# First layer from the fourth batch on as seven half-size products

## The chip, the cores and the metric

The kernel runs on one core of one Trainium2 chip. The metric is the device time of one execution in microseconds: the median of 3 runs before is 1244.26 us (1241.83 to 1246.42). Every time below is from the profiled execution, which has a time of its own.

## What is computed

Attention over 8 batches and 12 heads, with RMS-normed queries and keys, and then a two-layer network over all tokens:

```python
q_n, k_n = rmsnorm(q, g_q), rmsnorm(k, g_k)          # (8, 12, 448, 64)
attn = softmax(q_n @ k_n.T / sqrt(64))
x = (attn @ v)                                       # as (3584 tokens, 768)
h = x @ w_in                                         # (3584, 2048)
g = where(h > 0, h, exp(min(h, 0)) - 1)
return g @ w_out                                     # (3584, 768)
```

The inputs and outputs are float32.

## The kernel before

**Numbers in halves.** The matrix multiplies run on float16 operands. A float32 operand is kept as a high and a low half, and a product takes three matmuls into one bank: high by high, high by low, low by high. Weights are scaled by powers of two (`conv`, `conv_in`, `conv_out`, which run in the first 250 us or so beside the first two batches). First-layer weights stay on chip as `whi` and `wli`, 16 tiles each of six 128x128 blocks. High halves of the second layer stay as `whos`; its low halves go to DRAM (`wl_d`) and come back for every batch as `wls` (`wl_load`).

**Work of a batch.** A batch is 448 tokens. Attention of a batch has six pairs of heads, each with seven tiles of 128 rows of scores, 42 tiles. A tile T: `s_mm` makes scores in one of four banks (`t_s`; five in the first batch); DVE takes the maximum (`s_max`); ACT the exponential (`s_exp`); POOL, DVE, ACT and DVE turn it into two halves of probabilities `p` (`s_z`, `s_rec`, `s_hi`, `s_lo`; three buffers); SP transposes them by DMA into `ptall` (`s_tr`). After seven tiles `attend` multiplies a pair with v into the bank `av`, and `x_high` and `x_low` read from it one chunk of x in halves (a ring of nine chunks, `xs`). The network of batch b runs while attention of batch b+1 does (`mlp`). Its first layer makes 16 columns f of 128 features: 6 chunks x 3 matmuls of 448 tokens into one of three banks (`t_mo`: m0, m1 and s4); then the ELU steps of `m1_out`: an exponential on ACT, a subtraction and a maximum on DVE (which reads the bank last), and the halves `gall` by ACT and DVE. Its second layer makes six outputs d of 16 x 3 matmuls and reads each bank by ACT (`m2_out`). After the last batch's attention the network runs alone.

**The order.** No scheduler moves anything: a loop over half-steps h (two per tile, 84 per batch, HB) emits each step where the tables in SCHED put it, and each engine runs its own list in that order. From the third batch on the tables repeat a pattern. How many matmuls of the network are due by h is told by `due`, from the table "rate" and then at an even rate of 576 a batch. What couples the engines is the banks, the buffers named above and SP's single list of transfers.

```python
for i, (w, r) in enumerate(((wh, 0), (wh, 1), (wl, 0))):
    last = c == NC_ - 1 and i == 2
    nc.tensor.matmul(
        ph[:, :S], w[:, c, :], x[:, r, :], start=(c == 0 and i == 0), stop=last
    )
    yield m1_out(b, f, ph) if last else None
```

## Time and profile before

| | |
|---|---|
| median of 3 runs | 1244.26 us |
| profiled execution, its own time | 1245.14 us |
| span of the profile | 1243.4 us |
| mean granted TensorE clock | 0.995 |
| PE busy | 1188.5 us, 96%, 7180 matmuls |
| DVE, ACT, POOL busy | 866.0, 809.9, 498.9 us (70%, 65%, 40%) |
| DMA queue of SP | 413280 packets, 208.22 MB, 74.5% of 16 engines' span |

PE's row of the page counts a matmul from its first read to a modelled end, so two that follow each other overlap; a stage's pace is the distance of their starts. PEld is the weight load, which has a row of its own. "x288" and the like are counts. An arrow behind an idle time names what ended it. SPq is SP's own list: the time that an entry holds the list, not the time that the data takes.

### The profile page before, as it was taken

Reading aid. Unit: us, or ns where it says so; the run is one execution under the profiler, and the core shown is the slowest. Engines: PE = TensorE matmul, PEld = TensorE weight load, DVE = VectorE, ACT = ScalarE, POOL = GpSimd, SP = SyncE. Lnnn points to the kernel's source line nnn. Section 1 sums busy time; section 2 is a strip of 40 time slices with the busy share of each in tenths; the row PEclk is TensorE's granted clock in tenths of the full one; section 3 lists DMA queues with packets and bytes.
Section 4 is the critical chain, followed back from the end, with each engine's and each line's share of the span. In section 5 each row is a group of like instructions: output and inputs, shape, how many; then the busy total and the mean of one; then the engine's idle time right before and its main releaser. Section 6 shows DMA issues by size and latency. Waiting matters only on the chain.

```text
span 1243.4 us, 21717 instructions
## 1 busy us (share of the span) xinstructions
PE 1188.5 (96%) x7180; PEld 735.9 (59%) x7180; DVE 866.0 (70%) x2042; ACT 809.9 (65%) x1705; POOL 498.9 (40%) x789
## 2 busy tenths in 40 slices
PE   3878899999999999999999999999999999999998
...
GB/s 301 225 197 156 213 205 227 172 249 191 142 162 186 227 135 162 167 206 182 152 143 199 214 138 162 157 230 167 145 151 197 213 139 166 126 154 71 1 50 64
DMA packets 413393, 209.62 MB, mean 169 GB/s; under 512 B 369504, under 2 KB 389600, under 8 KB 413280
## 3 DMA queue, kind: packets, MB, share of 16 engines
q1 hardware_dynamic: 413280, 208.22, 74.5%
q8 instruction: 57, 0.93, 0.3%
...
## 4 chain that ended last, share of the span: by engine, by line
PE 77%; DVE 2%; DMA 2%; ACT 1%; issue 0%; POOL 0%; ACTq 0%
PE m L757 21%; PE m L743 21%; PE s L757 11%; PE s L743 10%; PE s L542 8%; PE av L635 7%; DMA ptall<-p 2%; DVE p L608 1%; ACT p L603 0%; ACT s L563 0%; DVE w32s L268 0%; DVE st L549 0%; DVE gall L692 0%; DVE w32s L314 0%; DVE e L679 0%
## 5 line engine op out<-in xcount | busy, mean ns | idle before, releaser
L549 DVE TENSOR_REDUCE st<-s 128x1 f32<-128x448 f32 x336 | 207.2, 619 | 158.7 <-PE s L542 156.3
L757 PE MATMUL m<-gall,whos 128*128 128x448 f16 x1024 | 282.0, 353 | 0.0
L567 POOL TENSOR_SCALAR st<-st 128x1 f32<-128x1 f32 x294 | 73.6, 250 | 488.6 <-ACT s L563 478.9
L757 PEld LDWEIGHTS <-whos 128*128 128x128 f16 x1536 | 221.7, 144 | 73.4 <-issue 0.7
L743 PE MATMUL m<-x,whi 128*128 128x448 f16 x926 | 256.0, 352 | 1.6 <-DVE x L649 1.2
L563 ACT ACTIVATE s<-s,st 128x448 f32<-128x448 f32 x294 | 178.1, 606 | 93.5 <-DVE st L549 90.3
L603 ACT ACTIVATE p<-s,st 128x448 f16<-128x448 f32 x294 | 185.1, 631 | 71.6 <-DMA ptall<-p 49.5
L743 PEld LDWEIGHTS <-whi 128*128 128x128 f16 x1536 | 149.7, 98 | 138.5 <-issue 3.6
L608 DVE SCALAR_TENSOR_TENSOR p<-s,st,p 128x448 f16<-128x448 f32 x294 | 198.5, 676 | 30.0 <-ACT p L603 29.2
L542 PE MATMUL s<-qkt 128*128 128x448 f16 (+1 forms) x768 | 185.4, 360 | 18.1 <-DMA qkt<-qkt 5.4
L757 PE MATMUL m<-gall,wls 128*128 128x448 f16 x512 | 181.3, 354 | 0.0
L743 PE MATMUL m<-x,wli 128*128 128x448 f16 x463 | 163.5, 353 | 0.0
L757 PE MATMUL s<-gall,whos 128*128 128x448 f16 x512 | 140.9, 353 | 0.0
L757 PEld LDWEIGHTS <-wls 128*128 128x128 f16 x768 | 110.6, 144 | 41.5 <-issue 6.8
L743 PE MATMUL s<-x,whi 128*128 128x448 f16 x450 | 124.0, 352 | 0.7 <-DVE e L679 0.7
L743 PEld LDWEIGHTS <-wli 128*128 128x128 f16 x768 | 75.1, 98 | 74.4 <-issue 7.0
L542 PEld LDWEIGHTS <-qkt 128*128 128x128 f16 (+1 forms) x768 | 63.3, 101 | 82.0 <-issue 36.8
L689 ACT ACTIVATE gall<-e,ui 128x448 f16<-128x448 f32 x128 | 85.1, 665 | 31.8 <-DVE e L684 31.8
L635 PE MATMUL av<-ptall,vt 128*64 128x448 f16 x924 | 96.9, 357 | 1.7 <-DMA ptall<-p 1.1
L692 DVE SCALAR_TENSOR_TENSOR gall<-e,ui,gall 128x448 f16<-128x448 f32 x128 | 87.7, 686 | 8.5 <-ACT gall L689 8.3
L387 POOL TENSOR_TENSOR nat<-nat,r 128x896 f32<-128x896 f32 (+1 forms) x48 | 84.5, 1760 | 22.3 <-DVE r L377 13.0
L757 PE MATMUL s<-gall,wls 128*128 128x448 f16 x256 | 90.6, 354 | 0.0
...
## 6 DMA issues: line engine op xcount, KB each, us to landing
wls<-wl_d SPq DMA_DIRECT2D x48, 512.0 KB, 4.1
...
raws<-in_w_out SPq DMA_DIRECT2D x24, 512.0 KB, 4.3
...
```

What stands on the lines that cost most here:

```text
L387: nc.gpsimd.tensor_tensor(out=n[:, a:], in0=n[:, a:], in1=r[:, a:], op=ALU.mult)
L542: nc.tensor.matmul(ps[r0 : r0 + n, :S], lhs, qq[:, 1, h * S : h * S + S], start=(t == 0), stop=(t == 2),)
L549: nc.vector.tensor_reduce(out=st[:, 0:1], in_=pss[T][:, :S], axis=AX.X, op=ALU.max, negate=True)
L563: nc.scalar.activation(e, ps, AF.Exp, bias=st[:, 0:1], accum_out=st[:, 1:2])
L567: (nc.vector if by_pe(T) else nc.gpsimd).tensor_scalar(out=st[:, 1:2], in0=st[:, 1:2], scalar1=1e-9, scalar2=2.0 ** (UP - 7) if by_pe(T) e ...
L603: nc.scalar.activation(p16[:, :S], pss[T][:, :S], AF.Copy, scale=stats[T][:, 2:3])
L608: nc.vector.scalar_tensor_tensor(out=p16[:, S:], in0=ps[:, :S], scalar=r, in1=p16[:, :S], op0=ALU.mult, op1=ALU.subtract)
L635: nc.tensor.matmul(av[64 * h : 64 * h + 64, :S], vs[:, h], ps[h], start=(k == 0), stop=(k == len(terms) - 1),)
L689: nc.scalar.activation(g[:, 0], e, AF.Copy, scale=ui)
L692: nc.vector.scalar_tensor_tensor(out=g[:, 1], in0=e, scalar=ui, in1=g[:, 0], op0=ALU.mult, op1=ALU.subtract)
L743: nc.tensor.matmul(ph[:, :S], w[:, c, :], x[:, r, :], start=(c == 0 and i == 0), stop=last)
L757: nc.tensor.matmul(py[:, :S], w, g[:, r, :], start=(f == 0 and i == 0), stop=last)
```

## The change

**Seven products.** From batch 3 (`FROM`), that is the fourth, the first layer is computed two columns at a time (`first`; eight pairs g). The 448 tokens are cut in two halves of 224, the six chunks of x in even and odd ones, and the two columns are the other cut of the weights, so that a pair is a 2x2 block product. It is made from seven products of sums of quarters instead of eight. A product is 3 chunk pairs x 3 terms of 224 tokens, 9 matmuls; two products share a bank (`ORDER7`), so a pair takes four turns of the three banks, and 63 matmuls. The rate table counts two of them as one.

**Adding them up.** `combine` reads each bank when it is done: two copies on ACT, five additions on DVE, two on POOL without a bank, into `quad` (two buffers) and `two` (one). The ELU steps then read from there, as they do in the first batch: the Relu is on ACT in place of the subtraction on DVE.

**Sums of x.** `x_even` and `x_odd` take the place of `x_high` and `x_low`: copies of `av` into `mix` by ACT, three subtractions on POOL for two chunks, and halves of seven pieces in place of four (448 and 1120 elements a row).

**Sums of weights.** `ratios` and `blocks` make, once, four sums of quarters for each pair, between half-steps 160 and 272 (batches 2 and 3 of attention). Two columns now share a scale, which adds a maximum of one column for every odd column while the weights are converted. High halves of three sums stay on chip (`wsum`); their low halves go to DRAM (`sl_d`) and are fetched for each product, 24 transfers of 96 KB a batch into four buffers (`fetch`), each behind the product that used the buffer last. The fourth sum replaces a quarter of `whi` and `wli` during batch 2's second layer (`fetch_sum`, 16 transfers).

**Tables.** From the third batch on, new tables give each step of a batch a place of its own ("tile+", "qk+", "v+", "mm+", "att+", "rate+"). The first layer of a batch now runs from half-step 12 to 50 of 84. After the last attention the steps advance every 3 counts in place of 7. Buffers of the conversion are put in one tile `work`, which the sums use afterwards.

```diff
 
     def t_s(T):
-        return sb[T % (5 if T < PB + 5 else 4)]
-
-    def t_mo():
+        return sb[T % (5 if T < PB + 5 else 4 if T < FROM * PB + PB else NSB)]
+
+    def t_mo(n=3):
         nonlocal taken
-        taken += 1
-        return mb[(taken - 1) % 3]
+        i = taken % n
+        taken = i + 1
+        return (mb + [sb[3]])[i]
...
-    xs = [const.tile([128, 2, S], F16, name=f"x{i}") for i in range(NX - 1)]
+    xall = const.tile([128, (NX - 1) * 2 * S], F16, name="xall")
+    xs = [t.rearrange("p (i s) -> p i s", i=2) for t in cols(xall, NX - 1)]
...
-    raws = const.tile([128, 2 * 2 * WI_W], U32, name="raws")
-    wts = const.tile([128, 2 * WI_W], F32, name="wts")
-    w32s = const.tile([128, 3 * WI_W], F32, name="w32s")
+    work = const.tile([128, 9 * WI_W], F32, name="work")
+    raws = work[:, : 4 * WI_W].bitcast(U32)
+    wts, w32s = work[:, 4 * WI_W : 6 * WI_W], work[:, 6 * WI_W :]
+    spare = const.tile([128, 8 * S], F32, name="spare")
 
...
+    NG, NK = NF // 2, NC_ // 2
+    w16, s16, x32 = work.bitcast(F16), spare.bitcast(F16), xall.bitcast(F32)
+    wsum = split(w16, 0, "u g k n", u=3, g=NG, k=NK, n=128)
+    wlow = [split(w16, (24 + i) * 384, "k n", k=NK, n=128) for i in range(4)]
+    stage = [split(w16, (24 + 5 * i) * 384, "u k n", u=5, k=NK, n=128) for i in range(2)]
+    f1, f2 = (split(spare, 768 * i, "e k n", e=2, k=NK, n=128) for i in range(2))
...
+    a = 28 * 384
+    pieces = [
+        [(piece(t, a, 2), piece(t, a + 2 * HS, 5)) for a in (z, z + 7 * HS)]
+        for t, z in ((s16, 16 * HS), (xall, 0))
+    ]
+    pieces.append([
+        (piece(w16, a, 2), piece(w16, a + 2 * HS, 5)), (piece(s16, 30 * HS, 2), piece(w16, a + 7 * HS, 5)),
+    ])
+    quad = [split(x32, (7 + 4 * i) * HS, "m q", m=4, q=HS) for i in range(2)]
+    two = split(ptall, 14 * HS, "m q", m=2, q=HS)
+    sh_d = [dram.tile([128, 2, NK, 128], F16, name=f"sh_d{g}") for g in range(NG)]
+    sl_d = [dram.tile([128, 3, NK, 128], F16, name=f"sl_d{g}") for g in range(NG)]
...
+    a_sum = const.tile([128, NF], F32, name="a_sum")
...
+            if width == WI_W and i % 2:
+                nc.vector.tensor_tensor(out=e, in0=e, in1=a_in[:, i - 1 : i], op=ALU.max)
...
+    def x_even(p):
+        m, k = mix, p % NPAIR // 2
+
+        def copy():
+            nc.scalar.activation(m[:, 0:3:2], av[:, :S].rearrange("p (i q) -> p i q", i=2), AF.Copy)
+
+        def one():
+            nc.gpsimd.tensor_tensor(out=m[:, 1], in0=m[:, 2], in1=m[:, 0], op=ALU.subtract)
+
+        return [copy, one, *parts(k, 0, m[:, 0:2])]
+
+    def x_odd(p):
+        m, k = mix, p % NPAIR // 2
+
+        def copy():
+            nc.scalar.activation(m[:, 3:5], av[:, :S].rearrange("p (i q) -> p i q", i=2), AF.Copy)
+
+        def one():
+            nc.gpsimd.tensor_tensor(
+                out=m[:, 5:7], in0=m[:, 4:5].broadcast_to([128, 2, HS]), in1=m[:, 1:3],
+                op=ALU.subtract,
+            )
+
+        def two():
+            nc.gpsimd.tensor_tensor(out=m[:, 7], in0=m[:, 5], in1=m[:, 3], op=ALU.subtract)
+
+        return [copy, one, two, *parts(k, 1, m[:, 3:8])]
+
+    def parts(k, i, x):
+        hi, lo = pieces[k][0][i], pieces[k][1][i]
+
+        def high():
+            nc.scalar.activation(hi, x, AF.Copy, scale=0.25)
+
+        def low():
+            nc.vector.scalar_tensor_tensor(
+                out=lo, in0=x, scalar=0.25, in1=hi, op0=ALU.mult, op1=ALU.subtract
+            )
+
+        return [high, low]
+
+    def neg(b):
+        return b == 0 or b >= FROM
...
         def two():
-            if b == 0:
+            if neg(b):
                 nc.scalar.activation(e, e, AF.Relu, scale=-1.0, bias=one_c)
...
+    def fetch(n):
+        g, u = divmod(n, 3)
+        nc.sync.dma_start(out=wlow[n % 4], in_=sl_d[g][:, u])
+
+    def fetch_sum(g, i):
+        nc.sync.dma_start(out=(whi, wli)[i][2 * g + 1][:, 0::2], in_=sh_d[g][:, i])
+
+    def weights(i, g, k):
+        if i < 4:
+            f, c = ((0, 0), (0, 1), (1, 1), (1, 0))[i]
+            return [t[2 * g + f][:, 2 * k + c] for t in (whi, wli)]
+        return [wsum[:, i - 4, g, k], wlow[(3 * g + i - 4) % 4][:, k]]
+
+    def first(b, wl_load):
+
+        def combine(g, bk, i):
+            h, t = quad[g % 2], two
+            r = part[:, g : g + 1]
+
+            def half(n, j):
+                return bk[n][:, j * HS : j * HS + HS]
+
+            def copy(j, scale):
+                nc.scalar.activation(t[:, j], half(0, j), AF.Copy, scale=scale)
+
+            def add(out, x, y, scale=None):
+                if scale is None:
+                    nc.vector.tensor_tensor(out=out, in0=x, in1=y, op=ALU.add)
+                else:
+                    nc.vector.scalar_tensor_tensor(
+                        out=out, in0=x, scalar=scale, in1=y, op0=ALU.mult, op1=ALU.add
+                    )
+
+            def add_up(out, x, y):
+                nc.gpsimd.tensor_tensor(out=out, in0=x, in1=y, op=ALU.add)
+
+            def elu(j):
+                return m1_out(b, 2 * g + j, h[:, 2 * j : 2 * j + 2].rearrange("p i q -> p (i q)"))[1]
+
+            row = SCHED["quad"][4 * g + i]
+            return row, [
+                [lambda: copy(0, r), lambda: copy(1, 1.0)],
+                [
+                    lambda: add(h[:, 0], half(2, 0), t[:, 0], r),
+                    lambda: add(h[:, 3], half(2, 1), t[:, 0]),
+                    lambda: add_up(h[:, 2], h[:, 3], t[:, 1]),
+                ],
+                [
+                    lambda: add(h[:, 1], half(3, 0), h[:, 2]),
+                    lambda: add(t[:, 0], half(3, 1), h[:, 3]),
+                    lambda: add_up(h[:, 3], t[:, 0], t[:, 1]),
+                    *elu(0),
+                ],
+                [lambda: add(h[:, 2], half(4, 0), t[:, 0], -0.25), *elu(1)],
+            ][i]
+
+        for g in range(NG):
+            if g in (4, 6):
+                wl_load(g // 2 - 2)
+            bk, n = {}, 0
+            for j, (i, slot, bank, side) in enumerate(ORDER7):
+                if bank not in bk:
+                    bk[bank] = t_mo(NMB)
+                o = bk[bank][:, side * HS : side * HS + HS]
+                q, z = (0, slot) if slot < 2 else (1, slot - 2)
+                for k in range(NK):
+                    wh, wl = weights(i, g, k)
+                    xh, xl = (pieces[k][y][q][:, z] for y in (0, 1))
+                    for m, (w, x) in enumerate(((wh, xh), (wh, xl), (wl, xh))):
+                        last = k == NK - 1 and m == 2
+                        nc.tensor.matmul(o, w, x, start=k == m == 0, stop=last)
+                        if last and i > 3 and 3 * g + i < 24:
+                            fetch(3 * g + i)
+                        n += 1
+                        if n == 63 or (n % 2 == 0 and (g % 2 or n < 62)):
+                            done = last and j in (1, 3, 5, 6)
+                            yield combine(g, bk, (j + 1) // 2 - 1 if j < 6 else 3) if done else None
+
+    def blocks(g):
+
+        st = stage[g % 2]
+        a11, a12, a21, a22 = (t[:, e] for t in (f1, f2) for e in (0, 1))
+        s1, s2, s3, s4 = (sums[:, i] for i in range(4))
+
+        def tt(out, x, y, op):
+            nc.gpsimd.tensor_tensor(out=out, in0=x, in1=y, op=op)
+
+        def join(i):
+            hi, lo = (t[2 * g + i].rearrange("p (k e) n -> p e k n", e=2) for t in (whi, wli))
+            tt((f1, f2)[i], hi, lo, ALU.add)
+
+        def common():
+            t = f1.rearrange("p e k n -> p (e k n)")
+            nc.scalar.activation(t, t, AF.Copy, scale=ratio[:, g : g + 1])
+
+        def flat(t):
+            return t.rearrange("p u k n -> p u (k n)")
+
+        places = (wsum[:, :, g], sums[:, :3], st[:, 2:]), (st[:, :1], sums[:, 3:], st[:, 1:2])
+
+        def cast(i):
+            hi, x, lo = places[i]
+            nc.scalar.activation(flat(hi), flat(x), AF.Copy, scale=0.25)
+
+        def rest(i):
+            hi, x, lo = (flat(t) for t in places[i])
+            nc.vector.scalar_tensor_tensor(
+                out=lo, in0=x, scalar=0.25, in1=hi, op0=ALU.mult, op1=ALU.subtract
+            )
+
+        def store(i):
+            if i:
+                nc.sync.dma_start(out=sh_d[g], in_=st[:, :2])
+            else:
+                nc.sync.dma_start(out=sl_d[g], in_=st[:, 2:])
+
+        return [lambda: join(0), common, lambda: join(1)] + [
+            lambda x=x: tt(*x)
+            for x in (
+                (s1, a21, a22, ALU.add), (s2, s1, a11, ALU.subtract), (s3, a11, a21, ALU.subtract),
+                (s4, a12, s2, ALU.subtract),
+            )
+        ] + [lambda i=i, f=f: f(i) for i in (0, 1) for f in (cast, rest, store)]
...
+        if b >= FROM:
+            yield from first(b, wl_load)
...
-            py = t_mo()
+            py = t_mo(3 if b < FROM else NMB)
             wl = wls.pop(d)
             for f in range(NF):
+                if b == FROM - 1 and d < 4 and f % 4 == 2:
+                    fetch_sum(2 * d + f // 8, f // 4 % 2)
+                if FROM <= b + 1 < B and d == NC_ - 1 and f % 4 == 0:
+                    fetch(f // 4)
...
-        put(hs[5:], [(x_high, p), (x_low, p)])
+        if p < FROM * NPAIR:
+            put(hs[5:], [(x_high, p), (x_low, p)])
+            continue
+        b, k = divmod(p, NPAIR)
+        put(
+            [h + HB * b for h in SCHED["x"][k]],
+            [(fn,) for fn in (x_odd if p % 2 else x_even)(p)],
+        )
...
+    put(SCHED["ratio"][0], [(ratios,)])
+    for g in range(NG):
+        put(SCHED["prep"][g], [(fn,) for fn in blocks(g)])
...
-        return n[i] if i < len(n) else int((h - START) * RATE)
+        if i < len(n):
+            return n[i]
+        a, r = divmod(h, HB)
+        u = SCHED["rate+"][0][r] - 100
+        plain = min(a - 1, FROM)
+        return plain * 576 + (a - 1 - plain) * 540 + (u * 576 // 540 if a <= FROM else u)
...
-        if done % 7 == 0:
+        if done % 3 == 0:
             h += 1
+            run_tasks(h - 0.5, 1)
...
+    "rate+": [
+        [20, 30, 40, 50, 51, 51, 52, 61, 71, 71, 82, 96, 100, 106, 107, 114, 118, 119, 131, 143,
...
+    "quad": [
+        [1, 0.5],
+        [1.5, 1, 2],
+        [1, 1, 2, 1.5, 1.5, 2.5, 5, 5.5],
+        [1, 2, 2.5, 4.5, 5, 8.5],
...
+    "prep": [
+        [160.5, 167, 162.5, 168.5, 171, 167, 172.5, 174, 175, 182, 175, 177, 182.5],
...
+FROM = 3
+NMB = 3
+NSB = 4
+ORDER7 = (
+    (0, 0, 0, 0), (4, 1, 0, 1), (1, 2, 2, 0), (5, 4, 2, 1), (3, 3, 3, 0), (6, 5, 3, 1), (2, 6, 4, 0)
+)
```

**SP in a first layer.** The list of transfers in the first layer of batch 4, before (L618 is a tile's transpose, L425 and L432 those of q and k, L343, L335 loads of v and of q and k; "waits" names the engine or queue waited for):

```order
L343 DMA vn<-in_v 128x512 [waits DMAHW7_49,Pool_49]
L618 DMA_TRANSPOSE ptall<-p_8394 128x7x64 [waits DMAHW0_49,DVE_49]
L618 DMA_TRANSPOSE ptall<-p_8394 128x7x64 [waits DMAHW1_49]
L618 DMA_TRANSPOSE ptall<-p_8428 128x7x128 [waits DMAHW2_49,DVE_49]
L425 DMA_TRANSPOSE qkt<-t_8374 128x7x128 [waits DMAHW3_49,PE_49,Pool_49]
L618 DMA_TRANSPOSE ptall<-p_8463 128x7x128 [waits DMAHW4_49,DVE_49]
L425 DMA_TRANSPOSE qkt<-t_8374 128x7x128 [waits DMAHW5_49,Pool_49]
L335 DMA nat<-in_qk 128x896 [waits DMAHW6_49]
```

The same place after (L658 is a tile's transpose, L464 that of q and k, L806 a fetch of low halves):

```order
L806 DMA work<-sl_d_142 128x384 [waits DMAHW5_49,PE_49]
L382 DMA vn<-in_v 128x512 [waits DMAHW6_49,Pool_49]
L658 DMA_TRANSPOSE ptall<-p_8907 128x7x128 [waits DMAHW7_49,DVE_49]
L806 DMA work<-sl_d_142 128x384 [waits DMAHW0_49,PE_49]
L658 DMA_TRANSPOSE ptall<-p_8884 128x7x128 [waits DMAHW1_49,DVE_49]
L806 DMA work<-sl_d_143 128x384 [waits DMAHW2_49,PE_49]
L464 DMA_TRANSPOSE qkt<-t_8848 128x7x128 [waits DMAHW3_49,Pool_49]
L806 DMA work<-sl_d_143 128x384 [waits DMAHW4_49,PE_49]
L806 DMA work<-sl_d_143 128x384 [waits DMAHW5_49,PE_49]
L374 DMA nat<-in_qk 128x896 [waits DMAHW6_49,Pool_49]
```

Fetches that wait for PE now stand between the transposes; nothing else left the list.

**DVE in the same first layer.** Before (L549 is a tile's maximum, L575 its reciprocal, L608 its low half, L673, L684 and L692 a column's ELU steps, of which L684 reads the bank):

```order
L692 SCALAR_TENSOR_TENSOR gall<-e,ui,gall 128x448 [waits Activation_49]
L673 TENSOR_SCALAR e<-e 128x448 [waits Activation_49]
L608 SCALAR_TENSOR_TENSOR p_8530<-s_69,st,p_8530 128x448 [waits DMAHW2_49,Activation_49]
L575 RECIPROCAL st<-st 128x1 [waits Pool_49]
L684 SCALAR_TENSOR_TENSOR e<-m_74,sc,e 128x448 [waits DVE_49]
L549 TENSOR_REDUCE st<-s_68 128x1 [waits PE_49]
L608 SCALAR_TENSOR_TENSOR p_8586<-s_70,st,p_8586 128x448 [waits DMAHW4_49,Activation_49]
```

After (L831 and L833 combine and read a bank, L763 is an ELU step that reads the sums, L589 and L648 are a tile's):

```order
L831 TENSOR_TENSOR xall<-m_74,xall 128x224 [waits PE_49,Pool_49]
L831 TENSOR_TENSOR ptall<-m_74,xall 128x224
L833 SCALAR_TENSOR_TENSOR xall<-s_71,ptall 128x224 [waits DVE_49,PE_49]
L615 RECIPROCAL st<-st 128x1 [waits Pool_49]
L648 SCALAR_TENSOR_TENSOR p_8977<-s_68,st,p_8977 128x448 [waits DMAHW3_49,Activation_49]
L589 TENSOR_REDUCE st<-s_67 128x1 [waits PE_49]
L589 TENSOR_REDUCE st<-s_70 128x1
L763 SCALAR_TENSOR_TENSOR e<-xall,ns,e 128x448 [waits Activation_49]
L831 TENSOR_TENSOR xall<-m_74,ptall 128x224 [waits PE_49,Activation_49]
```

Where one step read a column's bank, each bank now has one to two additions of 224, one of which waits for POOL's addition as well as for PE.

## Rows read from the trace of the kernel before

**Rows 1.** The page: busy us, share, instructions; PE in 40 slices, in tenths

```profile
PE 1188.5 (96%) x7180; PEld 735.9 (59%) x7180; DVE 866.0 (70%) x2042; ACT 809.9 (65%) x1705; POOL 498.9 (40%) x789
...
PE   3878899999999999999999999999999999999998
```

**Rows 2.** By stage: us; PE, PEld, DVE, ACT, POOL busy; clock, DMA share, GB/s

```profile
576.40:645.70 69.30, 69.30 (x406) 35.64 (x405) 56.74 (x131) 50.51 (x111) 28.52 (x46) 1.00 0.73 150
645.70:715.30 69.60, 69.60 (x404) 49.00 (x403) 41.31 (x99) 40.00 (x90) 27.97 (x50) 1.00 0.91 197
...
1130.20:1184.60 54.40, 54.40 (x290) 28.15 (x288) 26.16 (x46) 19.41 (x31) 0.27 (x1) 1.00 0.07 25
```

**Rows 3.** One line's instructions, last first layer: durations ns, first and last start

```profile
L743 PE MATMUL m<-x,whi x110: 352/352/353, 1130.2 to 1184.3; 128*128 128x448 f16 x110
...
L743 PE MATMUL m<-x,wli x55: 352/352/353, 1130.6 to 1184.5; 128*128 128x448 f16 x55
```

**Rows 4.** Timeline of PE, then of its loads: start, us, engine, line, count

```profile
63.55 0.52 PE L141 MATMUL m<-wts,ones 128*128 128x64 bf16 x12
63.90 0.19 PE L141 MATMUL m<-tiny,ones 128*128 128x64 bf16 x1
...
63.43 0.92 PEld L141 LDWEIGHTS <-ones 128*128 128x128 bf16 x26
```

**Rows 5.** By stage again, the densest 200 matmuls with loads

```profile
85.80:109.20 23.40, 22.32 (x201) 15.23 (x201) 21.67 (x59) 22.77 (x45) 18.32 (x19) 1.00 0.72 223
```

**Rows 6.** Groups on DVE in a first layer: busy us, mean ns, idle before

```profile
L608 DVE SCALAR_TENSOR_TENSOR p<-s,st,p 128x448 f16<-128x448 f32 x21 | 14.2, 676 | 1.3 <-ACT p L603 1.3
L549 DVE TENSOR_REDUCE st<-s 128x1 f32<-128x448 f32 x21 | 13.0, 620 | 7.6 <-PE s L542 7.4
...
L673 DVE TENSOR_SCALAR e<-e 128x448 f32<-128x448 f32 x15 | 5.8, 384 | 0.0
...
L150 DVE TENSOR_SCALAR vs<-p 128x1 int32<-128x1 int32 x1 | 0.2, 153 | 0.0
```

**Rows 7.** Groups on ACT in the same first layer

```profile
L603 ACT ACTIVATE p<-s,st 128x448 f16<-128x448 f32 x21 | 13.2, 629 | 3.6 <-DMA ptall<-p 2.4 <-ACT s L563 1.0 <-DVE st L575 0.2
...
L367 ACT ACTIVATE r<-ln 128x14 f32<-128x14 f32 x3 | 0.6, 215 | 0.1
```

**Rows 8.** Groups over the whole span, each form apart

```profile
L410 POOL TENSOR_TENSOR t<-nat,t 128x448 f16<-128x448 f32 x48 | 50.8, 1059 | 5.5 <-ACT t L396 2.6
...
L713 ACT ACTIVATE y<-m,ua 128x448 f32<-128x448 f32 x32 | 20.2, 633 | 36.4 <-PE m L757 34.2 <-DMA out<-y 1.2 <-DVE mv L179 0.8
...
L671 ACT ACTIVATE e<-e,one 128x448 f32<-128x448 f32 x16 | 10.6, 664 | 0.1
```

**Rows 9.** By stage again, while the weights are converted

```profile
160.00:200.00 40.00, 37.01 (x258) 20.00 (x257) 39.05 (x89) 36.75 (x74) 17.21 (x25) 1.00 0.91 205
200.00:240.00 40.00, 39.64 (x265) 24.69 (x264) 36.43 (x82) 37.70 (x75) 23.27 (x34) 1.00 0.88 200
```

**Rows 10.** Timeline around one column's bank (s): last matmul and last reader

```profile
588.05 0.35 PE L743 MATMUL s<-x,wli 128*128 128x448 f16 x1
...
591.84 0.68 DVE L684 SCALAR_TENSOR_TENSOR e<-s,sc,e 128x448 f32<-128x448 f32 x1
```

**Rows 11.** Timeline of SP's list: start, us, line, transfer

```profile
605.10 0.53 SPq L343 DMA_DIRECT2D vn<-in_v  x1
...
610.95 1.25 SPq L618 DMA_TRANSPOSE ptall<-p  x1
```

**Rows 12.** Transfers issued in a first layer, seven groups, KB and us to landing

```profile
ptall<-p SPq DMA_TRANSPOSE x25, 3.0
...
qkt<-t SPq DMA_TRANSPOSE x6, 3.4
```

**Rows 13.** Transfers issued in a second layer, eight groups

```profile
wls<-wl_d SPq DMA_DIRECT2D x4, 512.0 KB, 4.4
...
qkt<-t SPq DMA_TRANSPOSE x6, 3.3
```

180 lines of the change are left out of this document (154 added, 26 removed), and 21 rows, old and new, of the table SCHED.

## Prediction

> **What bounds the kernel now.** I read the busy shares first [rows 1]: PE is busy 96% of the span and in nearly every slice after the first fifth; no other engine passes 70%. Since the busy time of pipelined matmuls says little, I then read the stages of one batch [rows 2]. A first layer (576.4 to 645.7 us) and a second (645.7 to 715.3) each show PE busy all the time at granted clock 1.00; the first layer of the last batch, with no attention beside it, takes 54.4 us. Whether PE is truly full is told by the pace: there the matmuls begin, one after the other, from 1130.2 to 1184.5 us [rows 3], 54.3 us over 287 steps, 189.2 ns each. So every steady stage is PE's own streaming, and what is taken off PE there comes off the end as long as nothing else becomes late.
>
> **What the change takes off PE.** A first layer is 16 columns x 6 chunks x 3 terms = 288 matmuls of 448. The new one is 8 column pairs x 7 products x 3 x 3 = 504 matmuls of 224, each with a weight load of its own. The trace has no matmul of 224; its nearest rows lie on either side. The column sums stream 64 columns: 12 of them fill 0.35 us before the next group starts, 29.2 ns each, with 26 loads of 128x128 within the same 0.92 us [rows 4], so a load does not hold the pace there. The line through 29.2 (64 columns) and 189.2 (448) gives 29.2 + 160 x 0.4167 = 95.9 ns at 224. The new layer is 504 x 95.9 = 48.3 us, the old one 288 x 189.2 = 54.5: 6.16 us less a batch, **30.8 us** for batches 3 to 7. The unknown is whether PE is supplied with so many pairs of load and matmul for so long; the other end is 117 ns, the mean over 201 matmuls in 23.4 us [rows 5], a stretch in which waits set the pace too. I take 95.9, since 26 pairs at 29 ns are far below it.
>
> [...]
>
> **What it adds, and beside what.** A first layer with attention beside it lasts 69.3 us: 54.5 of its own and 14.8 of attention, for 21 tiles. The new rate table gives it 38 of a batch's 84 half-steps, so 19 tiles: 13.4 + 48.3 = 61.7 us of PE. What must the others do in that time?
>
> DVE: five combining operations of 224 for each pair. By length, between 0.153 us at one element and 0.676 at 448 [rows 6], one takes 0.41. Durations overlap (the 16 groups of this stage, 14.2 us the largest and 0.2 the smallest, add up to 65.4 us where the engine is busy 56.7), so they count 0.87: 40 x 0.41 x 0.87 = 14.3 us. Away go 16 steps of 0.384 (5.3, done by ACT now), three low halves of x (1.6, moved out of the stage) and two tiles (2.3): 56.7 + 14.3 - 9.2 = 61.8 us against PE's 61.7. The steps of the last two or three columns fall behind the stage's end, so 58 to 61 remain. ACT: 16 Relus of 0.664, and 16 copies of 224 at 0.42 by length between 0.215 and 0.633 [rows 7, 8], x 0.87 = 15.1, less two tiles and a part of x (3): 50.5 + 12 = 62.5, again with 3 to 8 us falling behind. POOL: 16 additions of about 0.6, half of 1.06 and a start [rows 8], on 28.5: far from full. So DVE and ACT go from 82% and 73% to about 95%. What that does to PE can be read elsewhere in the trace: at 200 to 240 us DVE is busy 36.4 and ACT 37.7 of 40 us and PE 39.6; at 160 to 200 DVE 39.05 and PE 37.0 [rows 9]. Between 1% and 7.5% of 61.7 us is 0.6 to 4.6 us a batch. I take 2.5, since DVE's load stands between the two: **10 us** for batches 3 to 6.
>
> The banks tighten too, and that is where such lateness reaches PE. In the column shown [rows 10] the last matmul of a bank starts at 588.05 and ends 0.35 later, and its last reader ends at 592.52, 4.1 us on; two other columns of 18 matmuls cover that. The new layer fills a bank with two products (2.4 us beside attention) and wants it back 3.6 to 4.8 us later. But its readers are now one or two short operations and not the ELU's three steps, so 2 to 3 us should do. I count it within the 2.5 us.
>
> SP: 31 transposes at 1.25 us and 15 plain transfers at about 0.55 [rows 11, 12] make 47 of 69.3 us. With 24 fetches of low halves it is 28 x 1.25 + 13.6 x 0.55 + 13.2 = 55.7 of 61.7 us, 90%; and each fetch stands in SP's order behind the product whose weights it overwrites, so the transposes queued behind it wait for PE. Who waits for those are ACT (three buffers of probabilities) and the pair's attend, two to four half-steps or 3 to 7 us later. That cover is thin but there: nothing on top of the 2.5. 2.4 MB more at the stage's 150 GB/s for 0.73 of the DMA engines [rows 2] is at most 11 us of them, so 0.73 becomes 0.93 to 1.0; at 200 to 240 us it was 0.88 and PE went on.
>
> Last batch: ACT and DVE both have about 4.8 us of durations a pair (two columns' ELU and the combining) beside 6.04 of PE; 1.5 us for waits, bounds 0 and 5. Preparing the sums: a pair costs POOL two joins of 768 (about 1.7, by 1.06 at 448) and four sums of 384 (0.95), 7 us; eight pairs 56 us, ACT about 20 and DVE 16, over some 170 us around batches 1 and 2 where each has more room than that: 2 us, bounds 0 and 5. Start: eight more maxima of one column, about 0.15 us each, while DVE is the bound: 1 us.
>
> Sum on the profiled execution: 1245.1 - 30.8 + 10 + 1.5 + 2 + 1 = 1228.8 us. It lay 0.9 us over the median, so **1228**.
>
> **Rivals.** (1) No waits: the 30.8 and the start's 1 us alone, 1214. For it: PE never idles in a steady stage now. Against: DVE and ACT at 95%. (2) DVE and ACT set the layer's length, as at 160 to 200 us: 4.6 us a batch (18.4), 4 in the last, 5 for preparing: 1242. (3) Slower: SP becomes the bound. The highest steady load that it carries now is the second layer's, 31 x 1.25 + 27 x 0.55 = 53.6 of 69.6 us [rows 13], 77%. It decides below 80%: 55.7 / 0.80 = 69.6 us is no shorter than today, and at 0.77 the layer lasts 72.3, 3.0 over; late transposes then hold the attends. 4 x 3.0 + 3 of preparing and start - 4.7 in the last batch: +10, so 1254. For it: every fetch waits for PE in the middle of transposes. Against: the 3 to 7 us of slack. (4) Also slower: supply at 117 ns a pair. Beside attention (504 + 107) x 0.117 = 71.5 us, 2.2 over today; the last batch 59.0, 4.5 over: 8.8 + 4.5 + 3 = +16, so 1260. For it: nothing denser and longer stands in the trace; against: 26 pairs at 29 ns. [...]
>
> **How the numbers follow.** Forecast 0.55, (1) 0.14, (2) 0.16, (3) 0.11, (4) 0.04. The forecast's own spread is mostly the 0.6 to 4.6 us a batch, 1219 to 1237. The range goes from 1214 to 1250 and takes in rivals 1 and 2 with it, a little over 0.8. A measurement of this kernel can tell about 0.5%, 6 us, from no change: faster (under 1238) 0.55 + 0.14 = 0.69, within 0.16, slower 0.15.
>
> **What would show it.** Right: the last batch's first layer at 48 to 50 us with a pace of 96 ns; those of batches 3 to 6 at 63 to 66 us with DVE and ACT over 90% busy, and PE's idle time before the first matmul of a bank, released by DVE or ACT; second layers still at 69 to 70. Wrong: a pace of 105 ns or more with no releaser named (4); attends waiting for ptall while SP has no gaps (3); second layers over 71 us, which would mean that attention's work was only pushed on; over 5 us of new idle PE before 450 us, which would be the preparation.

## The result: slower, 1258 us in place of 1243

The changed kernel takes 1258.32 us (median of 4 runs, 1254.28 to 1261.71) against 1243.20 (1241.83 to 1246.42) beside it: ratio 1.0117, 95% interval 1.0075 to 1.0158. I had forecast 1228, with 1250 as the upper end. The profiled execution of the changed kernel was its fastest, 1254.28 us with a span of 1252.5.

The page of the changed kernel, busy times and PE in 40 slices, answers to [rows 1]. Line numbers have moved: `s_mm` is L582, the plain first layer L966, the new one L874, the second layer L984.

```profile
PE 1167.9 (93%) x8260; PEld 835.8 (67%) x8260; DVE 956.1 (76%) x2195; ACT 919.1 (73%) x1919; POOL 664.7 (53%) x962
...
PE   3878799997999999999999999999999999999998
```

PE is busy 20.6 us less, and the span is 9 us longer. Three stages of it (a first and a second layer of batch 3, the last first layer) answer to [rows 2]: us; PE, PEld, DVE, ACT, POOL busy; clock, DMA share, GB/s.

```profile
591.40:658.00 66.60, 64.12 (x617) 55.49 (x616) 60.18 (x142) 58.32 (x131) 41.01 (x61) 1.00 0.89 172
658.00:731.30 73.30, 70.92 (x410) 49.49 (x408) 50.78 (x117) 50.57 (x109) 36.94 (x60) 1.00 0.98 206
1139.50:1194.20 54.70, 49.68 (x505) 48.34 (x504) 31.82 (x65) 32.04 (x59) 10.49 (x15) 1.00 0.20 61
```

The first layer got shorter by 3 us, the second longer by 4, and the last first layer, with no attention beside it and DVE and ACT busy for 58% of it, did not move: 54.7 us, before 54.5. In none of the three was PE busy all the time; before the change it was in all of them [rows 2].

Where the time went is read best by stages, from the first matmul of each to the first of the next. Four kernels of the experiments stand beside it: e1 has the new tables (with the shared scales and the faster steps at the end) and no seven products, e2 these tables and the preparing of sums, e16 the change with adding up cut short, e18 with most of the added work from batch 3 on cut short.

| us | before | change | e1 | e2 | e16 | e18 |
|---|---|---|---|---|---|---|
| first layer of batch 1 starts | 291.3 | 289.3 | 292.6 | 290.1 | 292.8 | 291.0 |
| batch 1, first layer | 76.7 | 88.1 | 87.0 | 88.2 | 88.8 | 86.2 |
| batch 1, second | 69.5 | 72.9 | 70.0 | 72.2 | 73.1 | 72.1 |
| batch 2, first | 69.4 | 69.0 | 69.0 | 69.6 | 69.0 | 69.2 |
| batch 2, second | 69.5 | 72.2 | 70.0 | 70.0 | 72.3 | 72.4 |
| batches 3 to 6, first (mean) | 69.4 | 66.3 | 69.1 | 69.1 | 65.3 | 63.2 |
| batches 3 to 5, second (mean) | 69.5 | 72.0 | 70.0 | 70.0 | 71.5 | 70.7 |
| batch 6, second | 67.6 | 66.9 | 66.9 | 66.8 | 66.9 | 66.9 |
| last first layer | 54.5 | 54.7 | 54.5 | 54.5 | 48.5 | 48.3 |

Added up from batch 1 on, tables cost +10.5 us (e1 less before), preparing +3.9 (e2 less e1), and the seven products with all that belongs to them bring -2.7 (change less e2). To be read with care: each column is one execution, and over the change and the kernels below that leave batch 1 as it is there, its first layer lies between 86.2 and 89.4, its second between 72.1 and 75.0 and its start between 289 and 294 us, so 2 or 3 us in one stage of batch 1 are no reading; later stages agree within 1 or 2.

### The profile page after: what moved, and what is told of

It is laid out like the page before. It is cut to its first block, busy times and chain, and to the rows that moved or that the text cites. A ratio compares the mean times of both kernels' runs of the same rounds, so it can differ in the third digit from the quotient of the medians.

```text
span 1252.5 us, 24746 instructions
## 1 busy us (share of the span) xinstructions
PE 1167.9 (93%) x8260; PEld 835.8 (67%) x8260; DVE 956.1 (76%) x2195; ACT 919.1 (73%) x1919; POOL 664.7 (53%) x962
## 4 chain that ended last, share of the span: by engine, by line
PE 40%; DVE 9%; ACT 8%; DMA 7%; issue 4%; POOL 1%; SPq 1%; ACTq 0%; DVEq 0%; POOLq 0%
PE m L984 13%; PE s L984 8%; DMA ptall<-p 5%; PE av L675 5%; PE s L582 4%; PE m L874 4%; PE m L966 3%; ACT p L643 2%; DVE p L648 2%; PE s L874 2%; PE s L966 2%; DVE e L763 1%; DMA qkt<-t 1%; DVE gall L776 1%; ACT e L751 1%
## 5 line engine op out<-in xcount | busy, mean ns | idle before, releaser
L984 PE MATMUL m<-gall,whos 128*128 128x448 f16 x1024 | 282.2, 353 | 2.9 <-DVE xall L833 2.6
L984 PEld LDWEIGHTS <-whos 128*128 128x128 f16 x1536 | 221.4, 144 | 74.8 <-issue 3.9
L648 DVE SCALAR_TENSOR_TENSOR p<-s,st,p 128x448 f16<-128x448 f32 x294 | 198.0, 676 | 95.1 <-ACT p L643 93.9
L589 DVE TENSOR_REDUCE st<-s 128x1 f32<-128x448 f32 x336 | 203.9, 614 | 43.5 <-PE s L582 43.3
L607 POOL TENSOR_SCALAR st<-st 128x1 f32<-128x1 f32 x294 | 74.5, 253 | 300.6 <-ACT s L603 284.9
L582 PE MATMUL s<-qkt 128*128 128x448 f16 (+1 forms) x768 | 183.6, 360 | 33.8 <-DVE p L648 18.7
L984 PE MATMUL m<-gall,wls 128*128 128x448 f16 x512 | 181.3, 354 | 0.0
L984 PE MATMUL s<-gall,whos 128*128 128x448 f16 x512 | 141.4, 353 | 0.9 <-DVE gall L776 0.7
L984 PEld LDWEIGHTS <-wls 128*128 128x128 f16 x768 | 110.8, 144 | 42.8 <-issue 8.2
L582 PEld LDWEIGHTS <-qkt 128*128 128x128 f16 (+1 forms) x768 | 63.1, 101 | 89.3 <-issue 55.7
L874 PEld LDWEIGHTS <-work 128*128 128x128 f16 x1080 | 103.5, 98 | 6.6 <-issue 1.4
L874 PEld LDWEIGHTS <-whi 128*128 128x128 f16 x960 | 92.6, 98 | 18.1 <-issue 12.4
L426 POOL TENSOR_TENSOR nat<-nat,r 128x896 f32<-128x896 f32 (+1 forms) x48 | 87.3, 1819 | 18.5 <-DVE r L416 13.7
L966 PE MATMUL m<-xall,whi 128*128 128x448 f16 x342 | 95.3, 352 | 1.9 <-DVE xall L689 1.5
L773 ACT ACTIVATE gall<-e,ui 128x448 f16<-128x448 f32 x128 | 83.6, 667 | 18.3 <-DVE e L768 9.6
L776 DVE SCALAR_TENSOR_TENSOR gall<-e,ui,gall 128x448 f16<-128x448 f32 x128 | 91.5, 725 | 2.8 <-ACT gall L773 2.3
L966 PEld LDWEIGHTS <-whi 128*128 128x128 f16 x576 | 56.2, 98 | 54.5 <-issue 5.4
L984 PE MATMUL s<-gall,wls 128*128 128x448 f16 x256 | 90.6, 354 | 0.0
L675 PEld LDWEIGHTS <-vt 128*64 128x64 f16 x924 | 55.2, 111 | 40.8 <-issue 6.5
```

Source lines behind the costliest of these rows:

```text
L426: nc.gpsimd.tensor_tensor(out=n[:, a:], in0=n[:, a:], in1=r[:, a:], op=ALU.mult)
L582: nc.tensor.matmul(ps[r0 : r0 + n, :S], lhs, qq[:, 1, h * S : h * S + S], start=(t == 0), stop=(t == 2),)
L589: nc.vector.tensor_reduce(out=st[:, 0:1], in_=pss[T][:, :S], axis=AX.X, op=ALU.max, negate=True)
L648: nc.vector.scalar_tensor_tensor(out=p16[:, S:], in0=ps[:, :S], scalar=r, in1=p16[:, :S], op0=ALU.mult, op1=ALU.subtract)
L675: nc.tensor.matmul(av[64 * h : 64 * h + 64, :S], vs[:, h], ps[h], start=(k == 0), stop=(k == len(terms) - 1),)
L773: nc.scalar.activation(g[:, 0], e, AF.Copy, scale=ui)
```

## Experiments: tables, preparing, fetches, banks

**Tables alone (e1) and with the preparing (e2).**

```diff
-FROM = 3
+FROM = 8
...
-                if b == FROM - 1 and d < 4 and f % 4 == 2:
+                if False and d < 4 and f % 4 == 2:
...
-    put(SCHED["ratio"][0], [(ratios,)])
-    for g in range(NG):
-        put(SCHED["prep"][g], [(fn,) for fn in blocks(g)])
```

(e2 without the last three lines.)

> All eight first layers stay plain, and nothing is prepared or fetched; what is left of the change is the new tables, the shared scales and the faster steps at the end. Theory A (preparing the sums costs what the stage from 288 to 377 us shows, +11.4 us against before): the time falls back to that of before, 1240 to 1246 us. Theory B (the new order itself costs it, 25 tiles of scores in that stage in place of 23): 1250 us or more. Last first layer 54.5 us in both.

> All first layers plain, but the sums of weights are made and stored as in the change, and then not used. Theory A: 11 to 16 us over the run without them, so 1253 to 1260 us, all of it before 450 us. Theory B: within 3 us of the run without them.

Measured: e1 1255.38 us (ratio 1.0099, 1.0070 to 1.0128), e2 1261.15 (1.0154, 1.0125 to 1.0184). Theory B: without a single one of the seven products the kernel is already about 12 us slower, and 10.3 of it lie in the first layer of batch 1. Preparing adds 4 (by stages) to 7 us (by the ratios), between what theories A and B gave e2. PE's timeline of the changed kernel there (start, us, line, tile, count, idle before and what ended it):

```profile
301.82 0.54 PE L966 MATMUL s<-xall,whi 128*128 128x448 f16 x2
302.63 0.54 PE L582 MATMUL s<-qkt 128*128 128x448 f16 x2 [0.27 <-DVE p L648]
304.57 0.54 PE L582 MATMUL s<-qkt 128*128 128x448 f16 x2 [1.40 <-DVE p L648]
307.40 0.54 PE L582 MATMUL s<-qkt 128*128 128x448 f16 x2 [2.29 <-DVE p L648]
308.21 0.71 PE L582 MATMUL s<-qkt 128*128 128x448 f16 x2 [0.27 <-DVE p L648]
308.72 0.58 PE L966 MATMUL s<-xall,wli 128*128 128x448 f16 x1
309.09 0.95 PE L966 MATMUL s<-xall,whi 128*128 128x448 f16 x2
```

Four tiles of scores stand in a row with no matmul of the network between them, and each waits for DVE to give back a bank. The place is a seam of two tables. The old rate table ends with 596 counts at half-step 178, and the new curve, which runs some 35 counts behind the old even rate, reaches 596 only at 185: so 0 matmuls in half-steps 179 to 184, where the kernel before has 7 in nearly each. In the window 300 to 320 us (before, then e1, then the change) that is

```profile
300.00:320.00 20.00, 20.00 (x116) 10.38 (x116) 17.61 (x40) 13.49 (x30) 8.64 (x13) 1.00 0.85 164
```

```profile
300.00:320.00 20.00, 16.05 (x67) 6.83 (x64) 12.16 (x29) 10.80 (x25) 6.83 (x11) 0.73 0.75 160
```

```profile
300.00:320.00 20.00, 15.45 (x81) 7.62 (x81) 18.20 (x36) 14.80 (x31) 16.28 (x18) 0.91 0.84 180
```

116 matmuls against 67 and 81. Part of it is the clock: the granted clock is 0.73 over these 20 us of e1 and 0.91 in the change, where the matmuls from 308.7 to 311.3 us, just behind the waits, start 0.37 us apart in place of 0.19 and the granted clock is 0.50. Over the whole layer e1's 10.3 us are 4.9 of waits (those of PE that have a releaser add up to 7.1 us, before to 2.2) and 5.4 of more busy time (79.9 us, before 74.5) for four matmuls more, at a granted clock of 0.92 in place of 0.98. In the change they are about 7 of waits and 4 of busy time, at 0.96.

**The seam spread evenly**, in the change (e5), in tables alone (e6) and in tables with preparing (e7):

```diff
-        return plain * 576 + (a - 1 - plain) * 540 + (u * 576 // 540 if a <= FROM else u)
+        w = plain * 576 + (a - 1 - plain) * 540 + (u * 576 // 540 if a <= FROM else u)
+        if a == 2:
+            w = max(w, 596 + (h - 179) * 460 // 72)
+        return w
```

> As the change, but where the old rate table ends and the new one has not caught up (half-steps 179 to 252, at 179 to 184 no matmul of the network stands between four tiles of scores) the network's matmuls are spread evenly. Theory G (this seam is what tables alone cost, +10.3 us in that stage): the first layer of batch 1 falls from 88 to 77 to 80 us, no slice with a granted clock below 0.9 after 300 us, and the time falls by 8 to 11 us, to 1247 to 1250. Theory B2 (the wait is only pushed on, because the attention's order is denser in all of that stage): a fall of 3 us or less.

> Tables alone (all first layers plain, nothing prepared), with the network's matmuls spread evenly over the seam. Theory G: 1242 to 1247 us, as before the change. Theory B2: above 1251 us.

> Sums of weights made and stored and not used, all first layers plain, matmuls spread evenly over the seam. The price of preparing without the seam is the difference to the tables alone with it: if the two make each other worse, more than the 6 us that they differ by with the seam; if preparing hides in what is then free of waits, 2 us or less; 4 to 6 us if it is a cost of its own (operations of the vector engine that last longer while the pool engine works).

Measured: e6 1251.07 us (1.0071, 1.0047 to 1.0094), with the first layer of batch 1 at 80.2 us in place of 87.0; e7 1269.93 (1.0211) with 94.0; e5 1263.71 (1.0168, 1.0137 to 1.0198) with 94.9. With the tables alone theory G gets two thirds of that stage and not its time, which was to be 1242 to 1247 us. And what it gets is the clock: in e6's layer it is 1.00, PE's busy time 74.1 us in place of 79.9, while the waits stay at 6.1 us, in e1 7.1. The same window of e6:

```profile
300.00:320.00 20.00, 18.20 (x109) 9.49 (x110) 16.05 (x39) 14.98 (x34) 7.19 (x13) 1.00 0.94 186
```

So in these two executions spreading took away the fall of the clock and hardly the waits. That DVE gives banks back late there comes with the new tables, spread or not (theory B2), and which of their steps does it was not separated. Once sums are prepared there, theory G fails: spread, the same place costs 6 to 7 us more, and preparing beside the spread seam costs 18.9 us (e7 less e6). The two make each other worse. PE's waits in that layer, in us in total, times, longest, of the change (289 to 377 us) and of e5 (287 to 383):

```profile
PE s L582 <- DVE p L648: 6.3, 7, 2.3
PE av L675 <- DMA ptall<-p: 1.8, 1, 1.8
```

```profile
PE s L582 <- DVE p L648: 11.3, 9, 2.2
PE av L675 <- DMA ptall<-p: 1.9, 1, 1.9
```

The clock is lower too, 0.93 over e5's layer against 0.96. The preparing's steps have their places for the seam as it stands; why moving the network's matmuls past them costs so much was not separated further.

**Fetches left out (e3), and four banks in the last batch (e4).**

```diff
-                        if last and i > 3 and 3 * g + i < 24:
+                        if False:
                             fetch(3 * g + i)
```

```diff
-                    bk[bank] = t_mo(NMB)
+                    bk[bank] = t_mo(4 if b == B - 1 else NMB)
...
-            py = t_mo(3 if b < FROM else NMB)
+            py = t_mo(4 if b == B - 1 else 3)
```

> As the change, but 20 of the 24 fetches of low halves of a Strassen batch are left out: those low halves are then wrong (four old ones are used again), everything else runs. Theory C (SP's list, with fetches that wait for PE between the transposes, is what holds PE in the steady batches): first layers of batches 3 to 6 fall from 66.3 to 63 us and second layers to 70, together 12 to 18 us, so 1240 to 1246 us. Theory D (the vector and scalar engines and the banks hold PE): within 3 us of the changed kernel, 1255 to 1261 us.

> As the change, but the last batch's network turns over four banks in place of three. Theory E (the turn of the banks costs the last first layer its 6.4 us): that layer falls from 54.7 to 49.5 to 51 us, the time by 4 to 5 us. Theory F (the steps of adding up are late by their order, a fourth bank only shifts it): 53.5 us or more, the time by 1 us or less.

Measured: e3 1258.61 us (1.0125), first layers 65.9 on average, second 72.1: theory C is out, and with it my rival of SP's list. e4 1257.21 (1.0113): by that layer theory E, it fell from 54.7 to 50.7 us; the time fell by 1.1 us, within the intervals, where E gave 4 to 5. One came back in the second layer (55.3 us from its first matmul to its last, in the change 54.3), which now waits 0.5 us for a column's halves. Why a bank matters with engines 58% busy shows the change's timeline, ACT first, then DVE, then PE:

```profile
1168.20 0.67 ACT L755 ACTIVATE e<-e,one 128x448 f32<-128x448 f32 x1
1168.78 0.43 ACT L827 ACTIVATE ptall<-m,part 128x224 f32<-128x224 f32 x1
1169.11 1.24 ACT L773 ACTIVATE gall<-e,ui 128x448 f16<-128x448 f32 x2
1170.26 0.34 ACT L827 ACTIVATE ptall<-m 128x224 f32<-128x224 f32 x1
...
1168.96 0.69 DVE L763 SCALAR_TENSOR_TENSOR e<-xall,ns,e 128x448 f32<-128x448 f32 x1 [1.56 <-ACT e L755]
...
1192.97 0.84 DVE L776 SCALAR_TENSOR_TENSOR gall<-e,ui,gall 128x448 f16<-128x448 f32 x1 [0.44 <-ACT gall L773]
1193.73 0.44 DVE L833 SCALAR_TENSOR_TENSOR xall<-m,part,ptall 128x224 f32<-128x224 f32 x1
...
1168.89 0.45 PE L874 MATMUL s<-work 128*128 128x224 f16 x3
1170.65 0.35 PE L874 MATMUL m<-spare,whi 128*128 128x224 f16 x2 [1.30 <-ACT ptall L827]
...
1194.22 0.54 PE L984 MATMUL m<-gall,whos 128*128 128x448 f16 x2 [2.63 <-DVE xall L833]
```

A bank is free after two copies on ACT (L827). Between them in ACT's list stand two high halves of `gall`, the ELU's (L773, 1.24 us), the second of which starts as DVE's L763 ends, and that had waited 1.56 us for ACT's Relu (L755). Nobody is slow, but PE waits 1.30 us for a copy that stands behind another column's ELU. The longest wait of the layer is of the same kind: at its end PE stands 2.63 us for a bank whose addition on DVE (L833) comes behind a low half (L776) that waited for ACT.

**Seam and four banks together, these in the first layer only (e8).**

> As the change, with the seam spread evenly and four banks for the last batch's first layer (not for its second). If the two gains add: 11 to 14 us under the changed kernel, 1244 to 1247 us, about the time of before.

Measured: 1261.47 us (1.0135, 1.0094 to 1.0175). The last first layer is at 50.8 again, and the time 2 us under that of e5, within both intervals; the seam's loss stays.

## Experiments: what holds PE beside the new work

**Preparing spread wider, one batch later (e9).**

```diff
-        put(SCHED["prep"][g], [(fn,) for fn in blocks(g)])
+        put([160.5 + (h - 160.5) * 1.75 // 0.5 * 0.5 for h in SCHED["prep"][g]], [(fn,) for fn in blocks(g)])
...
-FROM = 3
+FROM = 4
```

> Seven products from batch 4 on in place of batch 3, and the steps of preparing the sums spread over 1.75 times as many half-steps (160 to 356). Theory H (preparing costs because it is packed too densely): the second layer of batch 1 falls from 72.9 to 70 to 70.7 us and that of batch 2 from 72.2 to 70 to 70.7, preparing then costs 2 us or less; one batch fewer gains, 1 to 3 us: 1253 to 1257 us. If preparing costs the same however it is spread: 1259 to 1262.

Measured: 1269.40 us (1.0221, 1.0206 to 1.0236), 91.6 in the first layer of batch 1 and 73.7 in the second of batch 2; the second of batch 1 fell to 71.7. Theory H falls: spread out, the same steps cost more.

**Half of the preparing at a time**: without DVE's low halves (e10), without POOL's sums (e11).

```diff
-            hi, x, lo = (flat(t) for t in places[i])
+            hi, x, lo = (flat(t)[:, :, :1] for t in places[i])
```

```diff
         def tt(out, x, y, op):
+            out, x, y = (t[..., :1] for t in (out, x, y))
```

(Here and in e16, buffers that would be read unwritten are cleared once by POOL.)

> As the change, but of the low halves of the sums of weights the vector engine makes one element a row in place of all (so the sums' low halves are wrong). Against the tables alone, preparing costs 1.1 us in the first layer of batch 1, 2.9 in its second and 2.2 in the second of batch 2, 6.2 together. Theory I (it is the vector engine's own added work, 16 operations, 10.6 us for 9 of them): 4 us or more of the 6.2 go. Theory J (it is the pool engine's sums, beside which the vector engine's other operations last longer): 2 us or less go.

> As the change, but the pool engine's sums of weights' quarters are made for one element of each block (so the sums are wrong); casts, low halves, stores and fetches run in full. Theory J: the vector engine's operations of that stage go back to their lengths without preparing (gall 0.91 to 0.77 us, the subtraction of the ELU 0.65 to 0.47) and 4 us or more of the 6.2 go. Theory I: lengths go back, but 2 us or less of the 6.2 go.

Measured: 1259.83 us (1.0139, 1.0098 to 1.0180) and 1254.69 (1.0108, 1.0085 to 1.0132). Both have 85.0 in the first layer of batch 1 and 72.4 in the second of batch 2; the stages of batches 1 and 2 together lose 2.7 and 3.7 us of the change's 302.2. Neither reaches a theory's 4, and with the scatter of those stages the two can't be told apart. DVE's groups in that first layer tell what POOL does to DVE, e10 (POOL's sums in full) above, e11 (without them) below:

```profile
L648 DVE SCALAR_TENSOR_TENSOR p<-s,st,p 128x448 f16<-128x448 f32 x26 | 17.6, 679 | 5.1 <-ACT p L643 4.8
...
L776 DVE SCALAR_TENSOR_TENSOR gall<-e,ui,gall 128x448 f16<-128x448 f32 x13 | 12.1, 928 | 0.5 <-ACT gall L773 0.5
L757 DVE TENSOR_SCALAR e<-e 128x448 f32<-128x448 f32 x14 | 9.0, 643 | 0.0
```

```profile
L649 DVE SCALAR_TENSOR_TENSOR p<-s,st,p 128x448 f16<-128x448 f32 x26 | 17.6, 680 | 8.1 <-ACT p L644 7.9
...
L777 DVE SCALAR_TENSOR_TENSOR gall<-e,ui,gall 128x448 f16<-128x448 f32 x13 | 8.8, 676 | 0.0
L758 DVE TENSOR_SCALAR e<-e 128x448 f32<-128x448 f32 x14 | 7.0, 499 | 0.3 <-ACT e L752 0.3
```

Beside POOL's long sums a low half of `gall` lasts 928 ns and not 676, the subtraction 643 and not 499; the low half of `p`, which reads a bank, stays at 680. Why the first two are stretched and the third is not was not shown. My sum had POOL's time as cover and nothing for what it does to DVE. But the stage is equally long in e10 and e11, so the stretched steps are no full account either.

**Low halves of the network's values left out (e12).**

```diff
+            n = 1 if b >= FROM else S
-                out=g[:, 1], in0=e, scalar=ui, in1=g[:, 0], op0=ALU.mult, op1=ALU.subtract
+                out=g[:, 1, :n], in0=e[:, :n], scalar=ui, in1=g[:, 0, :n], op0=ALU.mult, op1=ALU.subtract
```

> As the change, but from batch 3 on the vector engine makes one element a row of the low halves of the network's middle values (so the output is less exact): 16 operations of about 0.68 us fewer a batch, 10.9 us of its 60 in a first layer of 66.3. Theory D (the vector engine's load holds PE in the steady batches): first layers of batches 3 to 6 fall to 63 to 64.5 us, second layers from 71.9 to 70 to 70.8, together 10 us or more; the last first layer to 51 to 53. Rival K (the order of banks and steps holds PE, not the load): 65.5 us or more, 71.3 or more.

Measured: 1253.55 us (1.0089, 1.0070 to 1.0108). First layers 65.8 on average, second 72.0, the last first layer 51.3: rival K in the steady batches, theory D in the last. The cut was smaller than expected, though: in the first layer of batch 3 DVE is busy for 56.2 us in place of 60.2. So K stands against 4 us less on DVE, and not 10.9.

**Steps moved: x's halves later (e13), the small softmax step on DVE (e14), that with the spread seam (e15).**

```diff
-        [63.5, 66, 66, 66.5, 68.5],
+        [63.5, 66, 66, 70, 72],
```

```diff
-        (nc.vector if by_pe(T) else nc.gpsimd).tensor_scalar(
+        nc.vector.tensor_scalar(
```

> As the change, but the halves of the pieces of x of every fourth pair (1120 elements a row) stand 4 and 3.5 half-steps later in the lists of the scalar and the vector engine, so that the scalar engine need not stand still for the pool engine's subtractions there (1.5 us in the trace of the change). Theory L (that stand is what the second layers of batches 2 to 5 give back): they fall from 72.2, 73.3, 71.6 and 71.1 to 70 to 71, together 4 us or more. Rival: 2 us or less.

> As the change, but the small step between exponential and reciprocal of every tile is on the vector engine (0.15 us, right ahead of the reciprocal) and no longer in the pool engine's list, where it stands behind additions of 1 to 2 us. Theory M (that step's delay is how the pool engine's added work reaches PE): the first layer of batch 1 falls from 88.1 to 85 to 86.5, its second from 72.9 to 71, the first layers of batches 3 to 6 from 66.3 to 64 to 65; 8 to 14 us in all. Rival N (the vector and scalar engines' own lists hold the tiles): 0 to 3 us, or slower, since the vector engine gets 42 x 0.15 = 6 us more a batch.

> As e14_sz, with the network's matmuls spread evenly over the seam. Theory M: the first layer of batch 1, 94.9 us with the spread seam and the step on the pool engine, falls to 80 to 84, and the time to 1240 to 1248 us. Rival N: 92 us or more.

Measured: e13 1267.78 us (1.0204, 1.0186 to 1.0222), second layers 73.7, 75.1, 74.7 and 72.7: longer, theory L's edit only made it worse. e14 1297.23 (1.0451, 1.0411 to 1.0491) and e15 1307.90 (1.0515): the first layer of batch 1 96.6 and 100.7, those of batches 3 to 6 69.7 and 69.4. Rival N, by far. DVE's waits in batch 1 of e14 (299 to 470 us), then one of the change there (289 to 450 us), and the first layer of batch 3 of e14 (the change's stands above):

```profile
DVE p L648 <- ACT p L643: 11.8, 17, 1.9
DVE st L589 <- PE s L582: 7.0, 7, 2.9
DVE st L607 <- ACT s L603: 5.3, 8, 2.1
```

```profile
DVE st L615 <- POOL st L607: 4.9, 5, 2.3
```

```profile
616.20:686.00 69.80, 64.62 (x618) 55.58 (x617) 63.79 (x159) 57.80 (x130) 34.22 (x39) 1.00 0.83 162
```

The step's wait is not what costs: DVE waits 5.3 us ahead of it now and waited 4.9 us for POOL's before. What grew is DVE's work: over batch 1 it is busy for 141.7 us of 170.9 in place of 132.7 of 161.0, so 9.1 of the 9.9 us more are busy time (6.5 the step itself, most of the rest other steps that last longer: in the first layer the subtraction 781 ns in place of 645, `gall`'s low half 950 in place of 905), and in the first layer of batch 3 3.6 us more go with 3.2 more of the layer. Added to DVE, work costs nearly its length here; taken off (e12) it gave little.

**Added work cut to one element a row**: adding up (e16), POOL's subtractions for x (e17), both with e3 and e12 (e18).

```diff
-                nc.scalar.activation(t[:, j], half(0, j), AF.Copy, scale=scale)
+                nc.scalar.activation(t[:, j, :1], half(0, j)[:, :1], AF.Copy, scale=scale)
...
             def add(out, x, y, scale=None):
+                out, x, y = out[:, :1], x[:, :1], y[:, :1]
...
             def add_up(out, x, y):
+                out, x, y = out[:, :1], x[:, :1], y[:, :1]
```

```diff
-            nc.gpsimd.tensor_tensor(out=m[:, 7], in0=m[:, 5], in1=m[:, 3], op=ALU.subtract)
+            nc.gpsimd.tensor_tensor(out=m[:, 7, :1], in0=m[:, 5, :1], in1=m[:, 3, :1], op=ALU.subtract)
...
```

(The other two subtractions alike.)

> As the change, but every step of adding up the seven products (two copies, five additions on the vector and two on the pool engine a pair) works on one element a row, so that the network's middle values are wrong; all waits and the order stay. Theory P (the length of the added work on the other engines holds PE): first layers of batches 3 to 6 from 66.3 to 63 to 64.5 us, the last from 54.7 to 49 to 51; second layers as they are. Theory Q (the places of the steps in the lists, whatever their length): 65.5 us or more, the last 53 or more.

> As the change, but the pool engine's subtractions for the pieces of x work on one element a row (so x's pieces are wrong). Theory L again (the scalar engine stands for them in the second layers): second layers of batches 2 to 5 from 72.2, 73.3, 71.6 and 71.1 to 70 to 71, together 4 us or more. Rival: 2 us or less, then it is the other steps for x or the denser lists as a whole.

> As the change, with the two edits before, one element a row of the network's low halves from batch 3 on, and 20 of 24 fetches left out (so the network's values are wrong). If the length of the added work is the cause, first layers fall to 62.8 to 63.5 us (48.3 + 14.5), second ones to 70 to 70.5 and the last first layer to 48.5 to 49.5: 25 us or so in all. If it is the places in the lists: 10 us or less.

Measured: e16 1245.57 us (1.0022, 1.0006 to 1.0039), e17 1259.84 (1.0134, 1.0097 to 1.0172; first layers 67.0, second 71.7, so L is out), e18 1234.32 (0.9941, 0.9921 to 0.9962), 24 us under the change. A steady first layer, a second and the last first layer of e18:

```profile
590.90:654.30 63.40, 63.23 (x618) 55.57 (x617) 48.87 (x143) 54.90 (x132) 28.70 (x63) 1.00 0.78 151
654.30:725.40 71.10, 70.48 (x409) 49.34 (x408) 48.42 (x114) 50.39 (x110) 31.45 (x59) 1.00 0.96 210
1122.50:1170.80 48.30, 48.30 (x505) 48.29 (x504) 16.61 (x67) 29.36 (x59) 3.33 (x15) 1.00 0.08 28
```

Theory P, but only for the whole: e16's first layers, 65.3, lie between what P and Q gave, its last first layer is P's. In steady first layers the fetches alone give 0.4 us, the low halves 0.5, adding up 1.0, the subtractions nothing; all together 3.1 of the 3.4 us that stand over PE's own (48.3 and 14.6 of attention, e1's 69.1 less 54.5). In the last layer adding up alone gives everything: 48.5. So PE's part of the prediction was right to 0.1 us.

No version here that does all the work beats the kernel before; e18, which leaves work out, is 0.6% faster.

## Why the prediction was wrong

Two steps failed. The sum had no term for the new tables and their seam with the old order, which cost 10.5 us; and it had the waits beside the new work too short, 11.8 us over in the steady batches and 4.9 in the last. Neither alone takes the sum out of the range: 1228.8 would have become 1239 with the first and 1245.5 with the second. Together they turn a gain into a loss.

**PE's saving: right.** 504 matmuls of 224 at 95.9 ns, 48.3 us, is what e16 and e18 show (48.5 and 48.3) over 504 pairs in a row, and the rival of 117 ns a pair is out.

**The tables: missing from the sum, +10.5 us.** I took from the tables how many half-steps a first layer gets and gave their seam with the old order no price. PE's list showed it without a chip: four tiles in a row where there had been 14 matmuls between two. I had named over 5 us of new idle PE before 450 us as the mark of the preparing; the mark came (PE's waits above), but most of it is there without the preparing, in e1. In the change itself tables and preparing act on the same stage, and 10.5 and 3.9 are one order of taking them apart; e5 and e7 show that they are not independent.

**Waits in steady batches: 2.5 us a batch, measured 3.4 in the first layer and 2.0 in the second.** The first layers lie at 65.7 to 66.6, at and just over the upper end of the 63 to 66 that I had given, with DVE at 90% and ACT at 88% where I had forecast about 95%. PE's own share of such a layer was 62.9 us and not my 61.7: of the 117 matmuls that ran in it beside its own 112 stayed, where 38 of 84 half-steps made me count 107. The second layers at 71.1 to 73.3 are what I had named as attention's work pushed on. Four batches: 4 x 3.4, and 8.2 in the second layers of batches 2 to 5, make 21.8 in place of 10. I had priced waits by DVE's busy share, from [rows 9]; the runs show that the share alone does not tell the price: 4 us less on DVE gave 0.5 (e12), 3.6 more cost 3.2 (e14), and only all cuts together free PE (e18).

**Last batch: 1.5 us, bounds 0 to 5; measured 6.4** (54.7 - 48.3), over the bound and all of the gain. I counted durations (4.8 beside 6.04 us a pair) and not the chain ACT, DVE, ACT that one bank's copies stand in. Its price is shown by e4, e12 and e16.

**Preparing: 2 us, bounds 0 to 5; measured 3.9 by stages,** 6.8 by the ratios of e2 and e1. Mis-sized; whether within its bounds the scatter leaves open. **The start: 1 us;** the first layer of batch 1 began 2.0 us earlier, in the scatter.

In sum: 1228.8 + 10.5 + 11.8 + 4.9 + 1.9 - 3.0 = 1254.9, the profiled 1254.3. The terms are read from stages of these traces, so that they add up shows only that no stage is left out; and the profiled execution is the fastest of four, 4 us under their median, which these terms do not explain. My rival (2), 1242 with 4.6 a batch, 4 in the last and 5 for preparing, was nearer in all three; with the tables added it comes to 1252.5. Open stays what the second layer of batch 2 gives back (2.2 us, in e18 too: the 16 fetches of sums and the first pieces of x both start there), why the seam spread hurts beside the preparing, and which steps of the new tables hold DVE in the first layer of batch 1.
